# Third weight pair behind attention's tail, casts and subtractions a block apart, expert weights landing over w_out's tiles

## The chip, the cores and the metric

One core of a Trainium2 chip runs the whole program. The metric is device microseconds of one execution, as the median of several. A profiled execution shows every engine: TensorE (PE; its weight loads are PEld), VectorE (DVE), ScalarE (ACT), GpSimd (POOL), SyncE (SP, which here only issues DMAs) and the 16 DMA engines.

## The reference

Three layers follow each other. Talking-heads attention (2 batches, 12 heads, 448 tokens, 64 wide) mixes the heads before and after the softmax; a gated feed-forward follows an RMS norm; a mixture of 8 experts with one expert per token ends it.

```python
scores = einsum('bhij,hg->bgij', scale * q @ k.T, w_pre)
attn   = einsum('bhij,hg->bgij', softmax(scores), w_post);  x = attn @ v      # [896, 768]
xn     = x / sqrt(mean(x*x) + 1e-6) * rms_g
x      = (silu(xn @ w_gate) * (xn @ w_val)) @ w_out                           # 768 -> 1536 -> 768
e      = argmax(x @ moe2_w_gate)
out    = gate * eom * (relu(x @ w1[e]) @ w2[e])                               # 768 -> 1024 -> 768
```

The feed-forward's weights are float64 in memory, everything else float32.

## The kernel before

Each large product is made of three fp32r matmuls: an operand is split into a high part (a cast on ScalarE) and a low part (a subtraction on VectorE that needs the cast), and high·high, high·low and low·high are added up in PSUM (`mm3`, lines 502 to 504).

**Attention** (`Attention.run`) walks over 90 blocks of 10 query rows by 12 heads, in 8 chunks. A step m of the loop does this: `pre(m)` (L172, PE) mixes the heads of a tile d that a DMA has shuffled out of the scores (`shuffle`, L166, issued five blocks ahead, from SP for even and from POOL for odd blocks); L176 (DVE) takes the row maximum; `soft` (L182, ACT) the exponential; `weigh(m-1)` (L189 to L191, DVE) scales the second mixing matrix; `post(m-2)` (L202, PE) mixes again and L204 (ACT) copies the result. Between them lie the score products of the next chunk (L157), the products with v (`av`, L216, copied to xT by L222), the norm of a finished chunk (L433 to L455), the loads of v of batch 0 (blocks 0, 2, .. 10) and of k of batch 1 (blocks 12 to 23), both issued from POOL, and whatever `beside` holds for a block. This order is written out by hand (`manual_schedule`); each engine runs its instructions in that order. What follows attention is laid out by a planner, which puts each instruction into its engine's queue by its own estimate of the time at which its inputs are there, and which may also put later work between attention's instructions.

**`beside`** holds the first weights. The weights of the feed-forward come in 12 pairs (gate and value, one pair fc = 128 of the 1536 columns). `f64_to_f32` turns a raw tile into float32: a DMA (L488), a shift (L489, DVE), an and-or (L490, DVE), a scaling (L493, ACT), a shift-or (L494, DVE). `split_one` (L526 cast, L527 subtraction) splits it. Pair 0 is done at blocks 58 to 67, pair 1 at 69 to 78, and at block 79 the DMAs of pair 2 are issued (`load_2`) into the raw tiles that pair 1 has left. The other steps of pair 2 are traced after attention, ahead of `ffn1(0, 1)`. At blocks 83 to 86 `split_x` (L475 cast, L476 subtraction) splits the first four chunks of the normed tokens.

**The tail** of attention has the last `av` products, the norm of the last chunk, the split of chunks 4 to 7, and as filling four products of the feed-forward that need only chunks 0 to 3 and pairs 0 and 1 (`fill`).

**The feed-forward** runs `ffn1(fc, g)` for 12 pairs by two groups of 448 tokens, then `ffn2` for seven tiles of 128 tokens against w_out, of which twelve raw tiles (`wor`) have been converted and split: pieces 0 and 1 live in `nw`, 2 and 3 in `w2p`, 4 to 7 in `w0`, 8 and 9 in `nw`, 10 and 11 in four of the `wor` tiles. `route` then does for each tile: transposes of y (L627), logits (L631), the argmax and a running count (L636 to L668 on DVE, L641 and L643 on PE), and a scatter of the tokens to `ys` (L670, POOL). For the last tile, `first_x` (L776) begins expert 0's transposed tokens out of what `ys` holds by then (`xe`, loaded on ACT's queue after the scatter before), and adds the last tile's own tokens with a picking matmul (L784) after the count.

**The experts**: eight steps of `mm1` and `mm2`. A weight comes as eight pieces of 768 KB (`feed`, L849, SP); 14 raw tiles (`raws`) take them in turn; `weights` casts (L865, ACT) and subtracts (L866, DVE) them. The memory of `raws`, `hi` and the rest is the memory that the feed-forward leaves. The pools lie one above the other in the order in which they are opened, in KB per partition: `nw` 24, `h0` 18, `h384` 12, `h640` 12, `wor` 36, `w2p` 12, `hs` 24, `y` 18; above `nw` the experts' pools begin again at the bottom: before the change raw0 to raw4 (3, 2, 2, 6 and 1 tiles of 6 KB), then `hi` (6 tiles). A load waits until the tiles below it have been read for the last time, and the planner puts it into SP's queue by when the pools below it are free, not by its turn.

Of the kernel before, what the change touches and what calls it, by code (L numbers as in the profile page):

```python
# [20 lines left out]
class Attention:  # L21
# [230 lines left out]
    def run(self):  # L252
        NCH, NB, SH, LP = len(self.chunks), len(self.blocks), self.SH, self.LP
        self.prologue()
        loads = {2 * j: f for j, f in enumerate(self.load_kv(0, "v"))}
        loads.update({j + 12: f for j, f in enumerate(self.load_kv(1, "k"))})
# [59 lines left out]
class Net:  # L316
# [152 lines left out]
    def split_x(self, t0, ni):  # L469

        nc, x = self.nc, self.xT[:, :, t0:t0 + ni]
        g = int(t0 >= self.groups[1][0])
        o = t0 - self.groups[g][0]
        xh, xl = (self.xs[g][:, j, :, o:o + ni] for j in range(2))
        nc.scalar.copy(xh, x)  # L475
        nc.vector.tensor_sub(xl, x, xh.bitcast(F32))  # L476
# [45 lines left out]
    def split_one(self, fc, f, nm, eng):  # L522

        t = (self.nw if fc % 2 else self.w0).tile([128, 2, self.KD, 128], F32R, tag="w" + nm, name=nm + "hl")
        h, l = t[:, 0], t[:, 1]
        self.nc.scalar.copy(h, f)  # L526
        eng.tensor_sub(l, f, h.bitcast(F32))  # L527
        return h, l

    def split_w(self, fc, ws):  # L530
        return [self.split_one(fc, f, nm, self.LO(self.nc)) for f, nm in zip(ws, "gv")]
# [89 lines left out]
    def route(self, t, y):  # L621
# [8 lines left out]
        for k in range(self.KD):  # L630
            nc.tensor.matmul(lg, lhsT=yT[:, k, :], rhs=self.rw[:, k, :], start=(k == 0), stop=(k == self.KD - 1))  # L631
        v, col = nc.vector, lambda j: m[:, j:j + 1]
# [282 lines left out]
    def run(self):  # L915
# [17 lines left out]
        def at(m, f):  # L933
            beside.setdefault(m, []).append(f)

        def first_weights(fc, slots, load=True):

            def begin():
                steps, fs = self.load_w(fc)
                for js, some, f, nm in zip(slots, steps, fs, "gv"):  # L940
                    some = some + [lambda f=f, nm=nm: ws[fc].append(self.split_one(fc, f, nm, nc.vector))]
                    for m, s in zip(js, some):
                        at(m, s)
            return begin

        def begin_x(g):
            self.xs.append(sp[g].tile([128, 2, self.KD, self.groups[g][1]], F32R, tag="s", name=f"x{g}"))
# [10 lines left out]
        def tail(avs, todo):  # L958
# [3 lines left out]
            late = [lambda c=c: self.split_x(c[0] * a.S + c[1], c[2]) for c in a.chunks[-4:]]  # L962

            def gen():
                n = 0
                while todo:
                    yield todo.pop(0)
                yield lambda: begin_x(1)
                yield from late[:3]
                yield from avs[:3]  # L970
                yield fill[0]
                yield from avs[3:]
                yield fill[1]
                steps = [s for s in todo]
# [5 lines left out]
                yield late[3]  # L980
            return gen()

        with ExitStack() as actx:
# [4 lines left out]
            at(57, first_weights(0, ((58, 61, 62, 63, 64, 65), (60, 63, 64, 65, 66, 67))))  # L988
            at(68, first_weights(1, ((69, 73, 74, 74, 75, 76), (70, 75, 76, 76, 77, 78))))
            at(79, load_2)  # L990
            at(80, lambda: begin_x(0))
            for j, c in enumerate(a.chunks[:4]):
                at(83 + j, lambda c=c: self.split_x(c[0] * a.S + c[1], c[2]))
# [18 lines left out]
        for some in raw2.pop():  # L1012
            for f in some:
                f()
# [41 lines left out]
        part = self.first_x(xs[0])  # L1056
        self.route(self.TT - 1, y)
# [7 lines left out]
        self.raws = []  # L1065
        for i, n in enumerate((3, 2, 2, 6, 1)):
            self.raws += [self.pool(m2, f"raw{i}", n)] * n
        self.raws = self.raws[7:13] + self.raws[:7] + self.raws[13:]
        self.nraw = 0
        self.hi = self.pool(m2, "hi", self.NHL)  # L1070
# [93 lines left out]
```

## Time and profile before

| | us |
|---|---|
| median of 3 runs | 786.6 (786.15 to 787.62) |
| profiled execution | 786.7 |
| its span | 785.0 |
| TensorE busy | 730.8 (93%) |
| VectorE busy | 479.8 (61%) |
| ScalarE busy | 387.5 (49%) |
| GpSimd busy | 78.0 (10%) |

By 40 slices of 19.6 us, the lines of the page that carry most (a digit is the busy share in tenths; PEclk the granted clock; DMA the busy share of 16 engines):

| | slices |
|---|---|
| PE | 7889999999998759999999998999988799999994 |
| DVE | 3555667566775775788888823032106889778750 |
| PEclk | 9999999999999799999999999999998899999998 |

A row of a timeline has the start, the duration, the engine, the line, the operation with output and inputs, and in brackets how long the engine had been idle and what ended that. A releaser is inferred from semaphore events. Busy time of TensorE is modelled at its end, since matmuls are pipelined.

### The profile page before, as it was taken

The numbers are of one execution on the slowest core, as the hardware profiler recorded it, in microseconds if no ns is written. First come the engines' busy times: TensorE is split into PE (matmuls) and PEld (weight loads), VectorE is DVE, ScalarE is ACT, GpSimd is POOL, SyncE is SP. The second block draws the span as 40 slices with busy tenths as digits, with TensorE's granted clock in tenths as the row PEclk, the third lists the DMA queues.
The fourth block names the chain that finished last, engine by engine and source line by source line (L and its number), as shares of the span: only waits on it lengthen the run. The fifth ranks groups of instructions, "written<-read, shape, count | busy, mean of one in ns | idle before, by whom it ended". The sixth has DMA issues, their size and how long they took to land.

```text
span 785.0 us, 11939 instructions
## 1 busy us (share of the span) xinstructions
PE 730.8 (93%) x4414; PEld 596.0 (76%) x4414; DVE 479.8 (61%) x1016; ACT 387.5 (49%) x679; POOL 78.0 (10%) x133
## 2 busy tenths in 40 slices
PE   7889999999998759999999998999988799999994
PEld 4456575665645538999999998999986688988894
DVE  3555667566775775788888823032106889778750
ACT  3455656556565453534334512232215777778661
POOL 5133100121001000000000000011000000020010
PEclk9999999999999799999999999999998899999998
DMA  8577755667566404795554000131159999999100
GB/s 136 105 157 147 121 73 82 120 121 173 86 145 113 86 5 161 205 284 195 185 176 163 1 1 0 45 138 61 41 192 387 378 380 381 380 342 355 58 25 17
DMA packets 83434, 122.02 MB, mean 155 GB/s; under 512 B 20915, under 2 KB 63559, under 8 KB 83375
## 3 DMA queue, kind: packets, MB, share of 16 engines
q1 hardware_dynamic: 75471, 98.05, 42.8%
q0 software_dynamic: 6752, 20.05, 12.3%
q10 hardware_dynamic: 1152, 3.15, 1.1%
q8 instruction: 36, 0.59, 0.3%
q14 instruction: 23, 0.19, 0.1%
HBM read 90.51 MB, written 12.21 MB: 131 GB/s over the span
## 4 chain that ended last, share of the span: by engine, by line
PE 66%; DMA 11%; DVE 9%; issue 7%; ACT 5%; POOL 0%; SPq 0%; POOLq 0%; DVEq 0%; ACTq 0%
PE ps_po L202 7%; PE ps_pm L172 6%; PE ps_pm L504 5%; PE ps_pm L502 5%; PE ps_pm L503 5%; PE ps_po L504 5%; PE ps_po L503 5%; PE ps_po L502 5%; PE ps_qk L157 4%; PE ps_av L216 4%; PE ps_qk L503 3%; PE ps_qk L504 3%; PE ps_qk L502 3%; DMA d<-s 3%; DMA xe<-ys 2%
## 5 line engine op out<-in xcount | busy, mean ns | idle before, releaser
L202 PEld LDWEIGHTS ps_po<-w,p 120*112 120x112 f32 x720 | 84.7, 180 | 68.6 <-issue 41.9
L866 DVE TENSOR_TENSOR wl<-raw,wh 128x1536 fp32r<-128x1536 f32 x64 | 110.9, 1754 | 28.2 <-ACT wh L865 28.1
L202 PE MATMUL ps_po<-w,p 120*112 120x120 f32 x720 | 94.9, 276 | 18.4 <-DVE w L191 17.1
L182 ACT ACTIVATE p<-ps_pm,mx 120x448 f32<-120x448 f32 x90 | 57.1, 634 | 102.9 <-DVE mx L176 62.0
L865 ACT CAST wh<-raw 128x1536 fp32r<-128x1536 f32 x64 | 93.0, 1481 | 7.6 <-PE ps_pm L504 4.7
L172 PE MATMUL ps_pm<-d,a_kpre 120*120 120x448 f32 x180 | 86.8, 564 | 4.9 <-DMA d<-s 4.9
L176 DVE TENSOR_REDUCE mx<-ps_pm 120x1 f32<-120x448 f32 x90 | 56.0, 622 | 49.7 <-PE ps_pm L172 49.0
L493 ACT ACTIVATE raw<-raw 128x768 f32<-128x768 f32 x36 | 33.0, 922 | 70.8 <-DVE raw L490 64.0
L204 ACT COPY at<-ps_po 112x480 f32<-112x480 f32 x90 | 50.9, 566 | 3.3 <-PE ps_po L202 1.1
L157 PE MATMUL ps_qk<-kt,qt 64*110 64x448 f32 (+2 forms) x192 | 52.1, 589 | 0.5 <-ACT qt L88 0.2
L503 PE MATMUL ps_po<-wl,hh 128*128 128x384 f32 x144 | 49.4, 343 | 0.3 <-DVE wl L866 0.2
L502 PE MATMUL ps_po<-wh,hh 128*128 128x384 f32 x144 | 49.2, 342 | 0.0
L504 PE MATMUL ps_po<-wh,hl 128*128 128x384 f32 x144 | 48.6, 340 | 0.1
L502 PE MATMUL ps_pm<-wh,xh 128*128 128x512 f32 x108 | 44.9, 416 | 3.0 <-ACT xh L828 2.2
L166 POOL DMA_DIRECT2D d<-s x42 | 24.7, 589 | 218.5 <-PE ps_pm L172 173.6
L504 PE MATMUL ps_pm<-wh,xl 128*128 128x512 f32 x108 | 44.1, 410 | 2.2 <-DVE xl L829 2.2
L216 PE MATMUL ps_av<-at,v 112*64 112x110 f32 (+2 forms) x768 | 45.0, 264 | 1.2 <-ACT at L204 0.7
L503 PE MATMUL ps_pm<-wl,xh 128*128 128x512 f32 x108 | 44.4, 411 | 1.5 <-DVE wl L866 1.5
L597 DVE TENSOR_TENSOR hl<-h,hh 128x1536 fp32r<-128x1536 f32 (+2 forms) x9 | 12.3, 1400 | 48.6 <-ACT hh L596 24.6
L216 PEld LDWEIGHTS ps_av<-at,v 112*64 112x64 f32 x768 | 37.0, 137 | 6.0 <-ACT at L204 0.9
L88 DVE COPY s<-ps_qk 110x448 f32<-110x448 f32 (+2 forms) x48 | 29.8, 622 | 14.8 <-PE ps_qk L157 13.8
L157 PEld LDWEIGHTS ps_qk<-kt,qt 64*110 64x110 f32 (+2 forms) x192 | 15.3, 174 | 30.5 <-issue 22.6
(258 smaller groups left out, 1589.1 us busy)
## 6 DMA issues: line engine op xcount, KB each, us to landing
raw<-in_moe_w_dram SPq DMA_DIRECT2D x64, 768.0 KB
d<-s SPq DMA_DIRECT2D x48, 210.0 KB
raw<-in_moe_w_gate_dram SPq DMA_DIRECT2D x12, 768.0 KB
raw<-in_moe_w_val_dram SPq DMA_DIRECT2D x12, 768.0 KB
raw<-in_moe_w_out_dram SPq DMA_DIRECT2D x12, 768.0 KB
d<-s POOLq DMA_DIRECT2D x42, 210.0 KB, 5.6
ys<-z SPq DMA_DIRECT2D x8, 385.0 KB
v<-in_v_dram POOLq DMA_DIRECT2D x12, 224.0 KB, 6.5
```

What stands on the lines that cost most here:

```text
L157: nc.tensor.matmul(pss[e][:ni], lhsT=self.qt[n][e * D:(e + 1) * D, p, :ni], rhs=self.kt[b, p][e * D:(e + 1) * D, :], start=True, stop=True,)
L172: self.marks[m, "p"] = nc.tensor.matmul(ps, lhsT=self.kpre.rearrange("p i g -> p (i g)"), rhs=self.dt.pop(m), start=True, stop=True).ins
L176: self.marks[m, "v"] = nc.vector.tensor_reduce(mx, ps, axis=AX.X, op=ALU.max, negate=True).ins
L182: self.nc.scalar.activation(p, ps, AF.Exp, bias=mx, scale=1.0, accum_out=sm)
L202: nc.tensor.matmul(ps[:, c], lhsT=p[:, c * CP:(c + 1) * CP], rhs=w, start=True, stop=True)
L204: self.marks[m + self.LP, "a"] = nc.scalar.copy(dst, ps.rearrange("p c h i -> p (c h) i")).ins
L216: nc.tensor.matmul(ps[e * D:(e + 1) * D, j, :ni], lhsT=vt[(g0 + e) // HH][:self.CP, (g0 + e) % HH, c, :], rhs=at[:, c, g0 + e, :ni], start ...
L502: nc.tensor.matmul(ps, lhsT=ah, rhs=bh, start=first, stop=False)
L503: nc.tensor.matmul(ps, lhsT=ah, rhs=bl, start=False, stop=False)
L504: self.last["t"] = nc.tensor.matmul(ps, lhsT=al, rhs=bh, start=False, stop=last).ins
L865: self.nc.scalar.copy(h, raw)
L866: self.last["v"] = self.nc.vector.tensor_sub(l, raw, h.bitcast(F32)).ins
```

## The change

- v's loads of batch 0 move from blocks 0, 2, .. 10 to 6, 8, .. 16; k's loads of batch 1 from blocks 12 to 23 to blocks 7, 9, .. 17 and 19 to 24.
- In `beside`, the cast of a weight and its subtraction stand in two consecutive blocks; pair 1's value ends at block 79. The split of the first four chunks is made likewise.
- In the tail the casts and subtractions of chunks 4 to 7 are spread between the products.
- The conversion of pair 2 is ordered on ScalarE behind the last cast and on VectorE behind the last subtraction of the tokens' split.
- In the last `route`, `first_x` runs behind the logits, not ahead of the transposes.
- The experts' pools: `hi` first, then raw0 to raw6 with 1, 2, 2, 2, 4, 2 and 1 tiles, used in the order 4, 0, 1, 2, 5, 3, 6. So expert 0's w1 lands over eight `wor` tiles (two of which hold w_out's piece 10), its w2 over the rest of `h0`, `h384` and the first half of `h640`, expert 1's w1 over `h640`, `w2p` and `wor`.

```diff
@@ -252,8 +252,9 @@
         self.prologue()
-        loads = {2 * j: f for j, f in enumerate(self.load_kv(0, "v"))}
-        loads.update({j + 12: f for j, f in enumerate(self.load_kv(1, "k"))})
+        loads = {2 * j + 6: f for j, f in enumerate(self.load_kv(0, "v"))}
+        for j, f in enumerate(self.load_kv(1, "k")):
+            loads[2 * j + 7 if j < 6 else j + 13] = f
         avs, todo, preps = [], [], []
...
@@ -472,8 +473,14 @@
         xh, xl = (self.xs[g][:, j, :, o:o + ni] for j in range(2))
-        nc.scalar.copy(xh, x)
-        nc.vector.tensor_sub(xl, x, xh.bitcast(F32))
+
+        def high():
+            self.last["xa"] = nc.scalar.copy(xh, x).ins
+
+        def low():
+            self.last["xv"] = nc.vector.tensor_sub(xl, x, xh.bitcast(F32)).ins
+
+        return high, low
...
@@ -523,12 +530,16 @@
         h, l = t[:, 0], t[:, 1]
-        self.nc.scalar.copy(h, f)
-        eng.tensor_sub(l, f, h.bitcast(F32))
-        return h, l
+        return [lambda: self.nc.scalar.copy(h, f), lambda: eng.tensor_sub(l, f, h.bitcast(F32))], (h, l)
...
     def split_w(self, fc, ws):
-        return [self.split_one(fc, f, nm, self.LO(self.nc)) for f, nm in zip(ws, "gv")]
+        out = []
+        for f, nm in zip(ws, "gv"):
+            steps, hl = self.split_one(fc, f, nm, self.nc.vector)
+            for s in steps:
+                s()
+            out.append(hl)
+        return out
...
@@ -618,7 +629,7 @@
-    def route(self, t, y):
+    def route(self, t, y, beside=None):
         nc, E, rp = self.nc, self.E, self.rp
...
@@ -629,6 +640,8 @@
             nc.tensor.matmul(lg, lhsT=yT[:, k, :], rhs=self.rw[:, k, :], start=(k == 0), stop=(k == self.KD - 1))
+        if beside:
+            beside()
         v, col = nc.vector, lambda j: m[:, j:j + 1]
...
@@ -938,8 +951,12 @@
                 for js, some, f, nm in zip(slots, steps, fs, "gv"):
-                    some = some + [lambda f=f, nm=nm: ws[fc].append(self.split_one(fc, f, nm, nc.vector))]
-                    for m, s in zip(js, some):
+                    def split(f=f, nm=nm, m=js[6]):
+                        (high, low), hl = self.split_one(fc, f, nm, nc.vector)
+                        ws[fc].append(hl)
+                        high()
+                        at(m, low)
+                    for m, s in zip(js, some + [split]):
                         at(m, s)
...
@@ -959,25 +976,31 @@
                     for fc, j, tag in ((0, 0, "qk"), (0, 1, "qk"), (1, 0, "qk"), (1, 1, "pm"))]
-            late = [lambda c=c: self.split_x(c[0] * a.S + c[1], c[2]) for c in a.chunks[-4:]]
+            def late(c):
+                return self.split_x(c[0] * a.S + c[1], c[2])
...
             def gen():
-                n = 0
                 while todo:
                     yield todo.pop(0)
-                yield lambda: begin_x(1)
-                yield from late[:3]
+                begin_x(1)
+                cs = [late(c) for c in a.chunks[-4:]]
+                yield cs[0][0]
+                yield cs[1][0]
                 yield from avs[:3]
+                yield cs[0][1]
                 yield fill[0]
+                yield cs[1][1]
                 yield from avs[3:]
+                yield cs[2][0]
+                yield cs[2][1]
                 yield fill[1]
-                steps = [s for s in todo]
+                steps = list(todo)
                 k = [s.__name__ for s in steps].index("mean") + 1
...
                 yield from steps[k:]
-                yield late[3]
+                yield from cs[3]
             return gen()
...
@@ -985,12 +1008,16 @@
             self.NCH = len(a.chunks)
-            at(57, first_weights(0, ((58, 61, 62, 63, 64, 65), (60, 63, 64, 65, 66, 67))))
-            at(68, first_weights(1, ((69, 73, 74, 74, 75, 76), (70, 75, 76, 76, 77, 78))))
+            at(57, first_weights(0, ((58, 61, 62, 63, 64, 65, 66), (60, 62, 63, 64, 65, 66, 67))))
+            at(68, first_weights(1, ((69, 73, 74, 75, 76, 77, 78), (70, 74, 75, 76, 77, 78, 79))))
             at(79, load_2)
...
             for j, c in enumerate(a.chunks[:4]):
-                at(83 + j, lambda c=c: self.split_x(c[0] * a.S + c[1], c[2]))
+                def split(c=c, j=j):
+                    high, low = self.split_x(c[0] * a.S + c[1], c[2])
+                    high()
+                    at(84 + j, low)
+                at(83 + j, split)
             with tc.manual_schedule():
...
@@ -1009,9 +1036,11 @@
             self.ffn1_out(fc, 0, early[fc, 0], early[fc, 1])
-        for some in raw2.pop():
-            for f in some:
-                f()
+        steps = raw2.pop()
+        with tc.issue_after(self.last["xa"]), tc.issue_after(self.last["xv"]):
+            for some in steps:
+                for f in some:
+                    f()
         self.ffn1(0, 1, ws[0])
...
@@ -1053,8 +1082,8 @@
         y, = self.ffn2(ts, hs)
-        part = self.first_x(xs[0])
-        self.route(self.TT - 1, y)
+        part = []
+        self.route(self.TT - 1, y, lambda: part.extend(self.first_x(xs[0])))
         self.warm(self.NW[2], self.last["t"])
...
@@ -1062,12 +1091,10 @@
         m2 = ExitStack()
-        self.raws = []
-        for i, n in enumerate((3, 2, 2, 6, 1)):
-            self.raws += [self.pool(m2, f"raw{i}", n)] * n
-        self.raws = self.raws[7:13] + self.raws[:7] + self.raws[13:]
+        self.hi = self.pool(m2, "hi", self.NHL)
+        self.raws = [[self.pool(m2, f"raw{i}", n)] * n for i, n in enumerate((1, 2, 2, 2, 4, 2, 1))]
+        self.raws = [p for i in (4, 0, 1, 2, 5, 3, 6) for p in self.raws[i]]
         self.nraw = 0
-        self.hi = self.pool(m2, "hi", self.NHL)
         self.xp = self.pool(m2, "xp", 2)
...
```

## Rows read from the trace of the kernel before

**Rows 1.** The page: the chain that ended last, by engine.

```profile
PE 66%; DMA 11%; DVE 9%; issue 7%; ACT 5%; POOL 0%; SPq 0%; POOLq 0%; DVEq 0%; ACTq 0%
```

**Rows 2.** Stages: us, PE PEld DVE ACT POOL busy, granted clock, DMA share, GB/s.

```profile
250.30:263.40 13.10, 5.40 (x24) 3.71 (x23) 6.71 (x14) 4.85 (x10) 0.58 (x1) 0.64 0.57 156
263.40:274.80 11.40, 10.87 (x127) 8.71 (x127) 7.82 (x25) 5.87 (x15) 1.15 (x2) 0.96 0.43 53
274.80:293.20 18.40, 10.47 (x62) 6.63 (x60) 13.54 (x40) 10.17 (x25) 0.00 (x0) 1.00 0.03 5
330.60:425.00 94.40, 94.40 (x468) 87.52 (x467) 80.30 (x121) 37.93 (x50) 0.00 (x0) 1.00 0.65 204
596.30:626.00 29.70, 23.72 (x107) 20.07 (x108) 26.83 (x27) 22.11 (x22) 1.73 (x1) 0.89 1.05 380
626.00:775.00 149.00, 148.26 (x784) 132.60 (x783) 108.52 (x126) 101.67 (x112) 13.00 (x8) 0.99 0.72 258
```

**Rows 3.** Timeline of TensorE, first blocks: start, us, line, operation, idle before and releaser.

```profile
37.41 0.98 PE L172 MATMUL ps_pm<-d,a_kpre 120*120 120x448 f32 x2 [0.15 <-DMA d<-s]
42.24 1.72 PE L172 MATMUL ps_pm<-d,a_kpre 120*120 120x448 f32 x2 [3.03 <-DMA d<-s]
```

**Rows 4.** Chain of waits, the same stretch: start, us, what.

```profile
31.45 10.66 DMA d<-s
```

**Rows 5.** DMA issues: queue, count, KB each, median us to landing.

```profile
v<-in_v_dram POOLq DMA_DIRECT2D x12, 224.0 KB, 6.5
k<-in_k_dram POOLq DMA_DIRECT2D x18, 112.0 KB, 6.5
```

**Rows 6.** Timeline of TensorE, attention's later blocks.

```profile
247.58 1.04 PE L202 MATMUL ps_po<-w,p 120*112 120x120 f32 x8 [0.51 <-DVE w L191]
250.31 0.98 PE L202 MATMUL ps_po<-w,p 120*112 120x120 f32 x8
259.75 1.91 PE L202 MATMUL ps_po<-w,p 120*112 120x120 f32 x8 [7.70 <-DVE w L191]
263.37 1.40 PE L202 MATMUL ps_po<-w,p 120*112 120x120 f32 x8
```

**Rows 7.** Timeline of VectorE, the same stretch.

```profile
256.32 0.56 DVE L489 TENSOR_SCALAR raw<-raw 128x768 uint32<-128x768 uint32 x1 [6.91 <-DMA raw<-in_moe_w_gate_dram]
```

**Rows 8.** Waits in 205 to 296 us: us in total, times, longest.

```profile
DVE x L476 <- ACT x L475: 5.2, 3, 2.2
```

**Rows 9.** VectorE by line, 200 to 430 us: busy us, mean ns.

```profile
L490 DVE SCALAR_TENSOR_TENSOR raw<-raw 128x768 uint32<-128x768 uint32 x35 | 33.3, 955 | 0.5
```

**Rows 10.** Timelines at attention's end: VectorE, then TensorE.

```profile
314.83 0.83 DVE L476 TENSOR_TENSOR x<-xT,x 128x648 fp32r<-128x648 f32 x1 [0.80 <-ACT x L475]
316.02 0.36 PE L502 MATMUL ps_pm<-x,ghl 128*128 128x448 f32 x1
```

**Rows 11.** Timeline of ScalarE and TensorE, from the last w_out tile to routing.

```profile
583.54 0.49 ACT L616 ACTIVATE y<-ps_po 128x384 f32<-128x384 f32 x1 [5.71 <-PE ps_po L504]
586.42 0.94 PE L776 MATMUL ps_pm<-ident,xe 128*128 128x128 f32 x6 [2.92 <-DMA xe<-ys]
588.92 1.51 PE L631 MATMUL ps_av<-rw,yT 128*128 128x16 f32 x12 [0.24 <-ACT yT L628]
591.41 0.17 PE L641 MATMUL ps_qk<-oh,tri 128*128 128x8 bf16 x1 [0.98 <-DVE oh L639]
```

**Rows 12.** Chain of waits: the load of expert 0's tokens.

```profile
578.88 7.50 DMA xe<-ys
```

**Rows 13.** Timeline of SyncE's queue, w_out's last matmuls.

```profile
577.80 0.37 SPq L849 DMA_DIRECT2D raw<-in_moe_w_dram  x1
583.53 0.90 SPq L849 DMA_DIRECT2D raw<-in_moe_w_dram  x2
```

**Rows 14.** Timeline of ScalarE, the first experts' start.

```profile
594.83 1.48 ACT L865 CAST wh<-raw 128x1536 fp32r<-128x1536 f32 x1
604.19 0.60 ACT L882 ACTIVATE h<-ps_pm 128x512 f32<-128x512 f32 x1 [3.39 <-PE ps_pm L504]
```

## The prediction, made before the changed kernel was seen

> **What bounds the kernel now.** I read the page's chain first, then the busy time by stage, then the timelines of the stretches that the diff touches. By the chain [rows 1] the end is TensorE's for two thirds, and it waits for DMAs for a tenth. By stage [rows 2] TensorE has no free time where no edit lies: it is busy for 94.40 of 94.40 us in the feed-forward (330.6 to 425) and for 148.26 of 149.00 among the later experts. So microseconds saved ahead of such a stage come out at the end, unless a feeder turns late. TensorE does idle where the edits lie: in the first blocks, at attention's blocks 80 to 89, and between the last w_out tile and the first expert. The stages [rows 2] show for the second of these 5.40 us busy of 13.10, then 10.87 of 11.40, then 10.47 of 18.40.
>
> **Part a, loads of v and k.** TensorE stands for 3.03 us ahead of pre(6) and then does it in 1.72 where pre(5) took 0.98 [rows 3]: 3.03 + 0.74 = 3.8 us. The transfer awaited took 10.66 us [rows 4]; issued in block 1, it shared the engines with the v loads of blocks 2 and 4 (224 KB each, 448 KB [rows 5]). These move behind block 6, so up to 3.8 us go. In return, blocks 6 to 11, which have three v loads before and after, get three k loads of 112 KB, 336 KB. If 448 KB cost 3.03 us of wait, 336 KB cost at most 3.03 x 336 / 448 = 2.3; they may be hidden altogether, since a block's d is asked for five blocks ahead. Bounds: a gain of 3.8, a loss of 2.3. I take 3.8 less two thirds of 2.3, 2.3 us. POOL's queue, past which these loads move, carries only its d shuffles there; v is first read in block 18, two blocks after its last load. The trace shows that a k load lands no sooner than a v load of twice the bytes (6.5 and 6.5 us [rows 5]). If k's 336 KB therefore count as 672, the cost is 3.03 x 672 / 448 = 4.5 and the term 3.8 - 4.5 = -0.7; that is in rival 3. The Trainium skill, "DMA: Bandwidth & Descriptors", section Specifications, has a rule of this kind: transfers under 512 B miss line rate, and a piece of k here is 64 floats, 256 B; by it the term would be the -0.7, and the equal landing times agree with it.
>
> **Part b, casts and subtractions of pairs 0 and 1.** A subtraction queued behind the same block's cast holds VectorE and, behind it, the scaling for which post waits. The post at 247.58 waited 0.51 us for that [rows 6]. Four such pairs: 0 to 2.0 us; I take 1.0. The added block costs only one block more of a raw tile's life; pair 2's value DMA waits for block 79's subtraction, with SP's d of block 86 behind it, needed seven blocks on.
>
> **Part c, pair 2's conversion out of attention.** The largest term. post starts at 250.31, and next at 259.75 after 7.70 us idle, and at half the granted clock, then at 263.37 [rows 6]; the clock of 250.3 to 263.4 is 0.64 on average [rows 2], so part of it was at the 1.2 GHz level after the idle time. The cause is one row of VectorE: L489 of pair 2 sat 6.91 us at the head of the queue for its DMA, the block's maxima and scalings behind it [rows 7]. Behind the tail that instruction cannot stand there. From 250.31 to 263.37 two blocks took 13.06 us; the block before took 250.31 - 247.58 = 2.73. Gain 13.06 - 2 x 2.73 = 7.6; bounds 6.9 (the wait alone) and 8.6 (blocks without the 0.51 wait). What is next late is the usual loop of maximum, exponential and scaling, which 2.73 contains.
>
> **Part d, blocks 81 to 83.** Pair 2's other steps go too, but each block here carries two av products and TensorE is busy for 10.87 of 11.40 us [rows 2]: 0 to 0.5, I take 0.4.
>
> **Part e, the first four chunks' split.** From 274.8 to 293.2 VectorE is busy 13.54 of 18.40 us and TensorE 10.47 [rows 2]. Three subtractions waited 5.2 us for their casts [rows 8], with the next maximum behind them. A block apart, VectorE becomes the limit: at most 18.40 - 13.54 = 4.9. Some of its idle time is the loop through ScalarE and stays: bounds 1 and 4.9, I take 3.2.
>
> **Part f, the tail and the feed-forward's start.** Pair 2 costs VectorE two shifts and four steps like L490 [rows 9], 2 x 0.56 + 4 x 0.955 = 4.9 us, and now comes after the last subtraction of the tokens (314.83 + 0.83 [rows 10]). Cover: from 316.02 [rows 10] TensorE does ffn1(0,1) and ffn1(1,1), 72 matmuls; at 468 in 94.40 us [rows 2] that is 14.5 us. In these VectorE has to do 4.9 plus two subtractions like L490, 1.9, together 6.8, and outputs. It is busy for 80.30 of 94.40 us later [rows 2], so the debt can be paid back within 33 us. Cost 0; without the cover 4.9. The spread casts of chunks 4 to 7 lie beside the filling products: 0. The last chunk's subtraction ends at 315.66, 0.36 us before it is needed, so the tail can neither gain nor lose much.
>
> **Part g, transposes behind logits.** After the last eviction of y (583.54 + 0.49 = 584.03) TensorE waits for xe until 586.42, and only then come first_x, transposes and logits (done at 588.92 + 1.51 = 590.43) and the count at 591.41 [rows 11]. first_x is 12 matmuls; transposes and logits then take 590.43 - 588.02 = 2.4 us if first_x ended 1.6 us after 586.42. Changed: transposes at 584.03, logits done at 586.4, first_x from then to 588.0, the count directly behind it, since its one-hot is ready 0.98 after the logits. 591.41 - 588.05 = 3.3 us; 4.0 if the planner puts the count first. xe took 7.50 us from its issue at 578.88 on [rows 12], on ACT's queue, beside the raw loads that SP had issued from 577.80 on [rows 13]. With the changed pools w2p's two loads and one of `wor` start in about these microseconds, three instead of two. A raw tile of 786 KB at 380 GB/s [rows 2] is 2.1 us. Low end 3.3 - 2.1 = 1.2. The Trainium skill, "DMA: Bandwidth & Descriptors", section Issuing engines are not separate DMA queues, says that a DMA started by ACT interleaves with SP's on the same 16 engines; by it the term would be the 1.2, and the 7.50 us agree that ACT's queue gives no way past.
>
> **Part h, expert weights.** SP's order in the trace is telling: the third expert load waited until 577.80 for w_out's piece 0, and expert 0's first pieces came behind it, most from 583.53 on [rows 13], though some of the memory was free long before. So I expect five loads ahead of ffn2's end over h0, h384 and h640, two over w2p, and expert 0's w1 again at about 583.5. That suffices: the first cast starts at 594.83 [rows 14], 591.5 after part g, and four tiles land at 2.1 us each by about 593; the fourth is cast last. Expert 0's w2 is there sooner, but ScalarE's cast of it stood behind the eviction of h at 604.19, idle for 3.39 us [rows 14], by the planner's order. I take 0; bounds -2.1 (the first pieces a tile later) and +3.4 (the idle time filled).
>
> **The sum.** 2.3 + 1.0 + 7.6 + 0.4 + 3.2 + 3.3 = 17.8 us. The profiled execution has 786.7 (span 785.0 and 1.7 around it), so 768.9; the median of the runs is 0.1 lower: 768.8.
>
> **Rivals.** (1) More: parts a and e at their upper ends and part h's idle time filled, 1.5 + 1.7 + 3.4 = 6.6 more, 762.2. For it: prefetched w2. Against: the order of casts is the planner's. Chance 0.10. (2) Pair 2 comes late: VectorE does other pairs' steps first, the cover fails, 4.9 us and a slow restart like 0.74 come back: 774.4. For it: 85% busy VectorE. Against: 14.5 us of cover for 6.8. Chance 0.13. (3) DMAs give back: part a -0.7 (a k load as dear as a v load), part g 1.2 (a third raw load beside xe), part h -2.1 (first pieces a tile later): 17.8 - 3.0 - 2.1 - 2.1 = 10.6, 776.0. For it: the k row [rows 5] and engines full at 380 GB/s [rows 2]; against: all three have to come. Chance 0.07. (4) It does not do what it says: the planner, laying out anew, puts another waiting step between the blocks, and b, c and e pay nothing: 6.0 less pair 2's 4.9 leaves 1.1, 785.5. Against: no other raw tile has its memory before attention's v is read. Chance 0.04. (5) Slower: VectorE, entering the feed-forward 4.9 us late, evicts products late throughout. Each of the 40 remaining groups of 18 matmuls would wait for an output queued behind one conversion step (0.955); at 0.6 us each that is 24 us, 786.6 + 6.2 = 792.8. It decides from 17.8 / 40 = 0.45 us per group. Against: 14 us of idle VectorE in 94. Chance 0.08.
>
> **Chances and range.** The forecast, 764 to 774, has 0.58. The range 761 to 779 takes in rivals 1 to 3 and the bounds of a, e and h. Faster by over 0.2% (about what a measurement of this kernel can tell from no change): forecast and rivals 1 to 3, 0.88; within 0.2%: rival 4, 0.04; slower: rival 5, 0.08.
>
> **What would show it.** Changed, pre(6) waits less than 1 us and blocks 6 to 11 show no wait for d (a); no idle time of several us on TensorE at block 80, and no L489 waiting for a DMA ahead of attention's last post (c); subtractions L476 without waits for L475 (e); attention's last post some 14 us earlier and ffn1 still without idle time (f); the count about 4.0 us after the last eviction of y, not 7.4 (g); seven expert loads issued before ffn2 ends (h). The prediction is wrong if TensorE idles where pair 2 is needed, if d waits reappear in blocks 6 to 17, or if the experts begin no sooner after the count.

## The result, and the profile after

The changed kernel takes 758.2 us (754.6 to 759.0); the kernel before, timed beside it, takes 787.0 (786.2 to 787.6). The ratio is 0.9626, interval 0.9593 to 0.9659. The profiled execution has 759.0 with a span of 757.3, so 27.7 us less than the span before. The forecast was 768.8, range 761 to 779: the direction was right, the size was 10 us short.

From the page after, the busy time and the chain by engine, which answers to [rows 1]:

```profile
PE 724.7 (96%) x4414; PEld 592.6 (78%) x4414; DVE 478.1 (63%) x1016; ACT 387.8 (51%) x679; POOL 77.3 (10%) x133
PE 72%; issue 9%; DMA 9%; DVE 7%; ACT 2%; POOL 0%; POOLq 0%; SPq 0%; DVEq 0%; ACTq 0%
```

TensorE does the same 4414 instructions as before. Of the 27.7 us, 21.6 are idle time of TensorE that went and 6.1 are busy time (730.8 before, 724.7 now); the mean granted clock is 0.989 against 0.975. The view by stages after, bounded by the same instructions as far as [rows 2] has them (post(77) to post(79), to post(82), to post(88), the feed-forward, the first expert, the rest; columns as there). The bound between the last two rows is not the same instruction as before; the table further down measures that stretch.

```profile
248.45:253.24 4.79, 3.83 (x24) 2.44 (x22) 4.45 (x11) 3.12 (x8) 1.12 (x2) 1.00 0.82 185
253.24:264.31 11.07, 10.54 (x126) 8.38 (x127) 5.84 (x23) 5.52 (x16) 0.60 (x2) 1.00 0.69 166
264.31:278.45 14.14, 10.28 (x62) 6.62 (x60) 13.27 (x40) 9.95 (x25) 0.00 (x0) 1.00 0.04 7
315.84:410.25 94.41, 94.41 (x468) 87.52 (x467) 82.40 (x125) 39.08 (x51) 0.00 (x0) 1.00 0.63 205
576.52:599.79 23.27, 21.58 (x106) 18.75 (x104) 21.71 (x26) 19.87 (x21) 0.00 (x0) 0.93 1.06 381
599.79:747.00 147.21, 147.04 (x788) 132.33 (x786) 113.34 (x132) 104.19 (x113) 13.84 (x9) 1.00 0.75 272
```

The first row was 13.10 us at a clock of 0.64 and is 4.79 at 1.00. The third was 18.40 and is 14.14, with VectorE busy for 13.27 of it: that engine is now the limit there. The feed-forward is unchanged, TensorE without idle time. The fifth row is the one that the prediction did not foresee: before, the first expert's stretch had 23.72 us of TensorE's work in 29.70, now 21.58 in 23.27.

The same in TensorE's timeline, for [rows 6] and [rows 11]: the posts behind the vanished stall, then the last tile's first_x and the count.

```profile
250.03 1.02 PE L202 MATMUL ps_po<-w,p 120*112 120x120 f32 x8
253.24 0.94 PE L202 MATMUL ps_po<-w,p 120*112 120x120 f32 x7 [0.84 <-DVE w L191]
568.34 0.49 PE L789 MATMUL ps_pm<-ident,xe 128*128 128x128 f32 x2 [0.44 <-DMA xe<-ys]
572.50 0.17 PE L654 MATMUL ps_qk<-oh,tri 128*128 128x8 bf16 x1 [0.98 <-DVE oh L652]
```

The post that waited for 7.70 us waits for nothing, the next one for 0.84, and the tokens' wait of 2.92 is 0.44.

Every other number on stages is the distance between the starts of the same two instructions in the timelines, TensorE's except for the eviction of y, which is ScalarE's. pre(m) and post(m) are block m's two mixings; "y to count" runs from the start of y's last eviction (583.54 before) to the count (591.41); "e0 to e1" from expert 0's first matmul (596.35) to the first matmul of the ninth group of expert 1's first product (631.50).

| run | pre 64 to 78 | pre 78 to 82 | pre 82 to post 89 | y to count | e0 to e1 |
|---|---|---|---|---|---|
| before | 41.8 | 20.3 | 27.7 | 7.9 | 35.2 |
| changed | 39.4 | 10.9 | 23.5 | 4.9 | 27.6 |
| changed_again | 39.4 | 10.9 | 23.5 | 4.4 | 27.0 |
| hold_alone | 41.8 | 14.5 | 27.7 | 7.2 | 35.1 |
| spacing_alone | 39.4 | 10.9 | 31.8 | 7.2 | 36.4 |
| new_pools_alone | 41.8 | 21.1 | 27.7 | 4.7 | 26.6 |
| pairs_close | 41.8 | 14.4 | 24.3 | 4.4 | 26.6 |
| pair2_free | 39.4 | 10.9 | 27.7 | 4.4 | 26.5 |
| tokens_close | 39.4 | 10.9 | 27.7 | 4.4 | 26.3 |
| first_x_early | 39.4 | 10.9 | 23.6 | 4.7 | 27.6 |
| early_loads | 39.4 | 10.9 | 23.5 | 4.4 | 27.6 |
| old_pools | 39.4 | 10.9 | 23.5 | 6.9 | 35.1 |
| old_pools_hold13 | 39.4 | 10.9 | 23.8 | 6.2 | 31.7 |
| old_pools_hold12 | 39.4 | 10.9 | 24.0 | 6.3 | 29.1 |
| old_pools_tokens_first | 39.4 | 10.9 | 23.5 | 6.4 | 28.7 |
| tokens_late | 39.4 | 10.9 | 23.5 | 4.4 | 28.8 |

The 27.7 us of the two profiled executions, in order: the start to pre(14) lost 1.2 (59.5 to 60.7), of which 1.9 lie ahead of pre(0), where nothing was edited (27.70 and 29.55), while pre(0) to pre(14) gained 0.6; pre(64) to post(89) gained 16.0; the tail and the feed-forward nothing (21.94 and 162.71 in both); the entry into w_out's products 1.1, which is the clock; y to count 3.0; from there to expert 0 0.9; e0 to e1 7.5; the rest 0.4.

### The profile page after: what moved, and what is told of

It is laid out like the page before. It is cut to its first block, busy times and chain, and to the rows that moved or that the text cites. A ratio compares the mean times of both kernels' runs of the same rounds, so it can differ in the third digit from the quotient of the medians.

```text
span 757.3 us, 11947 instructions
## 1 busy us (share of the span) xinstructions
PE 724.7 (96%) x4414; PEld 592.6 (78%) x4414; DVE 478.1 (63%) x1016; ACT 387.8 (51%) x679; POOL 77.3 (10%) x133
## 4 chain that ended last, share of the span: by engine, by line
PE 72%; issue 9%; DMA 9%; DVE 7%; ACT 2%; POOL 0%; POOLq 0%; SPq 0%; DVEq 0%; ACTq 0%
PE ps_po L202 8%; PE ps_pm L172 7%; PE ps_pm L511 6%; PE ps_pm L509 5%; PE ps_pm L510 5%; PE ps_av L216 5%; PE ps_po L511 5%; PE ps_po L509 5%; PE ps_po L510 5%; PE ps_qk L157 5%; DMA out_dram<-o,ids 4%; PE ps_qk L510 3%; PE ps_qk L511 3%; PE ps_qk L509 3%; DMA d<-s 2%
## 5 line engine op out<-in xcount | busy, mean ns | idle before, releaser
L879 DVE TENSOR_TENSOR wl<-raw,wh 128x1536 fp32r<-128x1536 f32 x64 | 110.9, 1753 | 21.6 <-ACT wh L878 21.5
L608 DVE TENSOR_TENSOR hl<-h,hh 128x1536 fp32r<-128x1536 f32 (+2 forms) x9 | 12.3, 1400 | 47.4 <-ACT hh L607 24.6
L88 DVE COPY s<-ps_qk 110x448 f32<-110x448 f32 (+2 forms) x48 | 29.8, 622 | 17.1 <-PE ps_qk L157 16.7
L157 PEld LDWEIGHTS ps_qk<-kt,qt 64*110 64x110 f32 (+2 forms) x192 | 15.2, 179 | 30.1 <-issue 24.0
```

The lines of the kernel that those rows point to most:

```text
L157: nc.tensor.matmul(pss[e][:ni], lhsT=self.qt[n][e * D:(e + 1) * D, p, :ni], rhs=self.kt[b, p][e * D:(e + 1) * D, :], start=True, stop=True,)
L879: self.last["v"] = self.nc.vector.tensor_sub(l, raw, h.bitcast(F32)).ins
```

## The experiments

Medians scatter: those of the kernel before, timed beside each batch, lie between 785.4 and 787.9. Where medians lie within 2 us of each other I go by the stages above, and say so.

**Pools undone in the changed kernel, and pools alone in the kernel before.**

```diff
-        self.hi = self.pool(m2, "hi", self.NHL)
-        self.raws = [[self.pool(m2, f"raw{i}", n)] * n for i, n in enumerate((1, 2, 2, 2, 4, 2, 1))]
-        self.raws = [p for i in (4, 0, 1, 2, 5, 3, 6) for p in self.raws[i]]
+        for i, n in enumerate((3, 2, 2, 6, 1)):
+            self.raws += [self.pool(m2, f"raw{i}", n)] * n
+        self.raws = self.raws[7:13] + self.raws[:7] + self.raws[13:]
+        self.hi = self.pool(m2, "hi", self.NHL)
```

> The changed kernel with the experts' pools laid out as before (raw0 to raw4 with 3, 2, 2, 6 and 1 tiles, hi above them); all else as changed. The changed kernel has 758.2 us. In its trace the stretch from the first expert's first matmul to the end is some 7.7 us shorter than before, where the prediction had 0. Theory order: the layout only makes the planner put expert 1's tokens (their transposes, casts and subtractions) ahead of a block of weight casts, so that TensorE neither waits twice for 2.2 us at expert 1's start nor falls to half clock there. Theory loads: the gain comes from weights that land earlier. Both expect the 7.7 us to be lost again: 765 to 767 us, with two waits of about 2 us on TensorE at expert 1's start. Theory elsewhere: the experts gained from the earlier scatter and routing, not from the pools: 758 to 760 us.

Measured 767.4 (765.5 to 768.6): 9.2 us lost.

> The kernel before (787.0 us) with only the experts' pools laid out as changed. Theories order and loads: the 7.7 us of the experts' stretch are gained alone, 778.5 to 780.5 us, with expert 1's tokens ahead of the casts and no wait of 2 us at its start. Theory elsewhere: within 1 us of the kernel before. A third outcome, more than 9 us gained, would say that the pools also pay ahead of the experts (routing).

Measured 776.5 (773.8 to 776.7) beside 787.9: 11.3 us gained, the third outcome. The pools are the largest part of the change, and they pay at two places: e0 to e1, and y to count. For the second, the chain of waits of the changed kernel:

```profile
559.59 3.47 DMA ys<-y,sl
563.08 5.22 DMA xe<-ys
```

The load of expert 0's tokens takes 5.22 us, not 7.50 [rows 12]. With the old pools two raw loads go out in the microsecond before it (558.90 and 559.37, the load itself at 559.71, in old_pools; 577.80 and 578.27 before, of which [rows 13] shows the first). With the new ones it is one, 0.2 us ahead (562.91 and 563.08), and in new_pools_alone none (579.53 against 579.37). The Trainium skill, "DMA: Bandwidth & Descriptors", section Issuing engines are not separate DMA queues, lets loads of all issuers interleave on the same engines; the two durations agree with that, and so do the other old-pool traces in which TensorE waits for this load (7.0 to 7.2 us). That the loads just ahead are the cause is read from the traces; no run changes them alone.

**Order or landing?** The same pools, once with expert 1's tokens ordered ahead, once with the new pools and the tokens ordered late.

```diff
 # old_pools_tokens_first, on top of old_pools
+        self.WB.update({n: ("ta", "tv") for n in (10, 11, 12, 13)})   # casts, subtractions behind the tokens'
+                if first and k0:                                        # expert 0's second product, second half
+                    s.enter_context(self.tc.issue_after(self.last["tp"]))
 # tokens_late, on the changed kernel
+                if p == 0:
+                    with tc.issue_after(self.last["t"]):
+                        nxt = self.transpose_x(xs[1], 1)
```

> As old_pools, and with an order written out for expert 1's tokens: the second half of expert 0's second product stands behind their transposes on TensorE, and casts and subtractions 10 to 13 of the weights stand behind theirs. Theory order: most of the 7.7 us comes back (the 5.5 us at expert 1's start), 759.5 to 761.5 us, no wait at expert 1's start. Theory loads: nothing comes back, 765 to 767 us or more, since TensorE or the casts then wait for weights or for the load of the tokens instead.

Measured 761.2 (758.5 to 761.9): 6.2 of the 9.2 us come back without any change of memory (1.5 of them in expert 0's first product, ahead of the edit, where the clock is 0.81 against 0.67 in old_pools).

> The changed kernel with the new pools, and expert 1's tokens ordered late on purpose: their transposes behind all of expert 0's second product, as the kernel before has them; the loads are as changed. Theory order: 4 to 6.5 us are lost against the changed kernel (762 to 764.7 us), with TensorE waiting for the tokens' cast and subtraction at expert 1's start. Theory loads: at most 1.5 us are lost, since weights are early either way.

Measured 756.6 (754.9 to 759.2), as much as changed_again in the same batch (756.7). By the stage 1.8 us are lost (28.8 against 27.0), not the expected 4 to 6.5, so my theory, as I had put it, fell: late transposes on TensorE are at most a small part of the cause. What differs shows on ScalarE. old_pools first, then tokens_late, then the changed kernel (timeline: casts of weights, evictions, then the cast of the tokens, L841):

```profile
591.10 8.36 ACT L878 CAST wh<-raw 128x1536 fp32r<-128x1536 f32 x6
599.37 0.58 ACT L920 ACTIVATE o<-ps_po,mt 128x384 f32<-128x384 f32 x1
599.84 0.86 ACT L841 CAST xh<-ps_qk 128x512 fp32r<-128x512 f32 x2
```

```profile
587.62 4.25 ACT L878 CAST wh<-raw 128x1536 fp32r<-128x1536 f32 x3
591.76 0.59 ACT L920 ACTIVATE o<-ps_po,mt 128x384 f32<-128x384 f32 x1
592.23 1.49 ACT L878 CAST wh<-raw 128x1536 fp32r<-128x1536 f32 x1
593.60 0.60 ACT L920 ACTIVATE o<-ps_po,mt 128x384 f32<-128x384 f32 x1
594.07 0.88 ACT L841 CAST xh<-ps_qk 128x512 fp32r<-128x512 f32 x2
```

```profile
592.18 1.50 ACT L878 CAST wh<-raw 128x1536 fp32r<-128x1536 f32 x1
593.57 0.87 ACT L841 CAST xh<-ps_qk 128x512 fp32r<-128x512 f32 x2
```

With the old pools six casts stand in a row and thirteen in all ahead of the tokens. With the new ones it is nine in the changed kernel, and twelve, broken up, in tokens_late. So the next theory was the queue, not the place on TensorE:

```diff
 # on top of old_pools; hold12: (12, 13)
+        self.WB.update({n: ("ta", "tv") for n in (13,)})
```

> As old_pools (767.4 us), and the thirteenth cast and subtraction of the experts' weights (the first of expert 1's second matrix) stand behind the cast and subtraction of expert 1's tokens; nothing is ordered on TensorE. In old_pools ScalarE has thirteen casts ahead of those tokens, six of them in a row (8.36 us), and VectorE thirteen subtractions; in tokens_late, where nothing was lost, it is twelve. Theory queue: one cast (1.48 us) and one subtraction (1.75 us) less ahead of the tokens take most of the two waits of 2.22 and 1.30 us at expert 1's start and the half clock behind them: 762.5 to 765 us. Theory loads: the time of the casts is set by the weights' landing, nothing comes back, 766.5 to 768 us.

> As old_pools_hold13, with the twelfth cast and subtraction behind the tokens too. Theory queue: no wait of over 1 us is left at expert 1's start unless its own last weights come late; 760.5 to 763.5 us, as old_pools_tokens_first (761.2), though the transposes stay late on TensorE. Theory loads: 766.5 us or more.

Measured 765.7 (765.0 to 768.1) and 763.7 (761.3 to 767.6). Both medians lie 0.2 to 0.7 us off the expected bounds, high; between 767.4 and 763.7 the ranges overlap, so the stages decide: e0 to e1 falls from 35.1 to 31.7 and to 29.1. The waits of TensorE at expert 1's start show why, old_pools above, hold12 below:

```profile
600.48 0.79 PE L509 MATMUL ps_pm<-wh,xh 128*128 128x512 f32 x1 [2.22 <-ACT xh L841]
603.85 0.80 PE L511 MATMUL ps_pm<-wh,xl 128*128 128x512 f32 x1 [1.30 <-DVE xl L842]
```

```profile
600.10 0.50 PE L510 MATMUL ps_pm<-wh,xh 128*128 128x512 f32 x1 [0.46 <-ACT xh L842]
601.96 0.50 PE L512 MATMUL ps_pm<-wh,xl 128*128 128x512 f32 x1 [0.23 <-DVE xl L843]
```

In the first, the matmuls start at half clock as well (0.79 us each where the second has 0.50). Holding back two casts and two subtractions gives 6.0 of the 7.5 us, while no order was set for the transposes and the loads stay late. Of these 6.0, 1.2 lie in expert 0's first product, ahead of the edit, and are the clock there (0.81 against 0.67). From the start of expert 0's second product to the end of e1, where the edit acts, old_pools has 21.8 us, hold13 19.9, hold12 17.1 and the changed kernel 15.0: the queue makes 4.8 of 6.8 us. The Trainium skill, "TensorE: Matmul & The Clock Gate", section Architectural detail: the array is 16× 32×32, not 1× 128×128, says that ScalarE and VectorE take their queues strictly in order; these rows agree.

**Pair 2 and the pairs' spacing**, each undone in the changed kernel and each alone in the kernel before. Some conversion steps of the pairs move by a block with the spacing (their block numbers are left out of the cut), so the two are tested together.

```diff
 # pair2_free: without the order        # hold_alone: this order alone, in the kernel before
-        with tc.issue_after(self.last["xa"]), tc.issue_after(self.last["xv"]):
 # pairs_close: cast and subtraction in one block      # spacing_alone: a block apart, in the kernel before
-                        at(m, low)
+                        low()
```

> The changed kernel without the order that holds pair 2's conversion behind the tail; the planner puts it where it wants. Theory (the prediction's part c): it comes back between attention's last blocks, its first shift sits at the head of VectorE's queue for its DMA, TensorE idles for 6 to 8 us at block 80 and runs at half clock after: 758.2 + 8.5 = 766.7, between 765 and 768 us. Rival: with casts and subtractions a block apart VectorE has so much room that the conversion costs little, 759 to 761 us; the order matters little then.

Measured 759.8 (758.3 to 763.7): the rival's time. The stall is gone from pre(78) to pre(82) even so. The planner now puts the first shift behind the next maximum and scaling, where it waits for less (VectorE, pair2_free):

```profile
253.52 0.56 DVE L496 TENSOR_SCALAR raw<-raw 128x768 uint32<-128x768 uint32 x1 [1.97 <-DMA raw<-in_moe_w_gate_dram]
```

What the order behind the tail is worth then shows one stage on, where VectorE is the limit: 23.5 becomes 27.7.

> The changed kernel with cast and subtraction of weight pairs 0 and 1 in one block again (pair 1's value ends at block 78); pair 2 still held behind the tail. In the trace of the changed kernel the spacing gained 2.4 us at blocks 65 to 70 and 0.7 at block 77, where the prediction had 1.0 for all. Theory wait (the subtractions waited 1.5 and 2.7 us, the prediction took one post's 0.51): 758.2 + 3.1 = 761.3, between 760 and 762.5 us, and no stall at block 80. Theory place (the spacing, not the order behind the tail, takes pair 2's stall away, as pair2_free suggests): the stall at block 80 returns as well, 768 to 770 us.

Measured 766.4 (760.7 to 768.9), between the two theories: 2.4 us at pre 64 to 78 as expected, and 3.4 more at pre 78 to 82.

> The kernel before (785 to 788 us) with only pair 2's conversion ordered behind the tail; casts and subtractions of the pairs stay in one block. Theory of the prediction (part c): all of the stall at block 80 goes, 8.5 us from block 78 to block 82, 778 to 780 us. Theory two waits (from pairs_close): behind the shift that waits 6.91 us for its DMA stands the subtraction of pair 1's value, which would have waited 2.6 us for its cast anyway; 5.9 us go and a wait of 2.2 us stays ahead of a post, 780 to 782.5 us.

Measured 779.0 (775.5 to 782.7) beside 787.7. The median speaks for the first theory, the trace for the second: 20.3 becomes 14.5, not 10.9, and this wait is left (VectorE, hold_alone):

```profile
252.33 0.96 DVE L527 TENSOR_TENSOR vhl<-raw,vhl 128x768 fp32r<-128x768 f32 x1 [2.62 <-ACT vhl L526]
```

It explains 5.8 us of the gain; the others (0.7 at y to count, 1.1 behind it) fall where nothing was edited and are not put down to it.

> The kernel before with only casts and subtractions of pairs 0 and 1 a block apart; pair 2's conversion free. Theory of the prediction (part b): 1 us (0 to 2), and the stall of 7.7 us at block 80 stays: 785 to 787 us. Theory wait: 2.4 us at blocks 65 to 70 and 0.7 at block 77 whatever pair 2 does; and since pair 1 ends a block later the planner puts pair 2's first shift later too, behind the maximum and scaling of a block, so that it waits some 2 us for its DMA, not 6.9 (as in pair2_free): 5 to 9 us gained in all, 777 to 782 us.

Measured 778.1 (777.6 to 781.4) beside 787.7, as the second theory has it. The stall goes wholly (20.3 to 10.9), and 4.1 us come back behind it, in the stretch at whose head pair 2's steps now lie (27.7 to 31.8; VectorE does them from 253.3 to 261.9 us, the tokens' subtractions from 266.9 on).

**The tokens' spacing undone.**

```diff
                     high()
-                    at(84 + j, low)
+                    low()
```

> The changed kernel with cast and subtraction of the first four chunks of the tokens in one block again (blocks 83 to 86). Theory of the prediction (part e, 3.2 us, 1 to 4.9; 4.3 in the trace): 758.2 + 4.3 = 762.5, between 761 and 763.5 us, with waits of the subtraction for its cast, 1 to 2.2 us each. Rival: the gain there came from pair 2's steps being gone from blocks 79 to 83 and ScalarE being early; then at most 1.5 us are lost, under 760 us.

Measured 761.6 (758.6 to 764.2), 3.4 us lost; in the stage 23.5 becomes 27.7, 4.3 us.

**first_x and the loads undone.**

```diff
 # first_x_early
-        part = []
-        self.route(self.TT - 1, y, lambda: part.extend(self.first_x(xs[0])))
+        part = self.first_x(xs[0])
+        self.route(self.TT - 1, y)
 # early_loads
-        loads = {2 * j + 6: f for j, f in enumerate(self.load_kv(0, "v"))}
-        for j, f in enumerate(self.load_kv(1, "k")):
-            loads[2 * j + 7 if j < 6 else j + 13] = f
+        loads = {2 * j: f for j, f in enumerate(self.load_kv(0, "v"))}
+        loads.update({j + 12: f for j, f in enumerate(self.load_kv(1, "k"))})
```

> The changed kernel with first_x ahead of the last tile's transposes again. Theory order (the prediction's part g): the transposes wait for the tokens' load once more, 3.3 us (1.2 to 4.0) are lost, 760 to 762 us. Theory load: with the new pools fewer raw loads are issued just ahead of that load; it takes 5.2 us, not 7.5, and lands about when y is there, so the order is worth at most 0.5 us: 757.7 to 759 us. The trace of new_pools_alone, which has the early first_x and no wait for the tokens, speaks for it.

Measured 759.8 (757.8 to 762.0). The stage says 4.7 against 4.4 to 4.9: the order is worth nothing that can be seen once the pools are new (with the old ones, 0.3 to 0.9: 7.2 against 6.2 to 6.9).

> The changed kernel with v's and k's loads issued where they were before (v in blocks 0 to 10, k in 12 to 23). The prediction gave the move 2.3 us (-2.3 to 3.8). Theory load (the prediction's part a): block 6's tile d shares the engines with v's loads, so the wait ahead of its first mixing grows from 2.58 back to 3 us or more and 1 to 2.5 us are lost: 759 to 761 us. Theory shuffle: the tile's own transfer takes 10.0 us even with no other load beside it in the changed kernel (10.66 before), so the move is worth at most 0.6 us and the time stays at 757.5 to 759; the distance from block 0 to block 14 is 31.2 to 31.8 us either way, unless the clock falls at another point.

Measured 759.0 (758.0 to 761.1), 0.7 above the changed kernel of the first batch and 2.2 above changed_again, which is not more than the scatter. The chain of waits, changed kernel and early_loads:

```profile
33.34 10.00 DMA d<-s
```

```profile
31.93 10.68 DMA d<-s
```

**The changed kernel once more.**

> The changed kernel once more, to see how far its stretches differ between executions: the same order of work, so the distances between events after block 14 should agree within 0.2 us except where the granted clock falls at another place; the start (to block 14) may differ by up to 4 us, as among the runs so far. Median 757 to 760 us.

Measured 756.7 (754.3 to 760.0), 0.3 below the expected bound. The stages of the table agree within 0.1 up to post(89), within 0.7 behind it; the start to pre(14) is 57.3 against 60.7, and the entry into w_out's products 15.2 against 12.3.

## Why the prediction was wrong, point by point

**h, the step that failed.** The prediction took 0 for the experts, with +3.4 as its upper bound, "the idle time filled", and argued against more that "the order of casts is the planner's". It is the planner's, but the planner lays out anew when a pool moves. With the new pools nine casts stand ahead of expert 1's tokens, not thirteen, and 7.5 us went from e0 to e1. All of it went from the start of expert 0's second product on (22.9 us before, 15.0 now); there the queue makes 4.8 of the 6.8 us that the pools are worth in the changed kernel (old_pools_hold12). Weights that come sooner gained nothing at expert 0: nine expert loads are issued before ffn2's last matmul, four before the change, and its first product, up to its ninth group, takes 9.8 us against 9.4. The bound was wrong for a second reason: it was taken from one idle time of ScalarE. The row for the stage, which the text quoted for its GB/s alone, had 29.70 us with TensorE busy for 23.72 at a clock of 0.89 [rows 2], so 6 us idle and a slow clock besides. The same kernel's timeline has 4.4 of them at expert 1's start:

```profile
620.52 0.50 PE L502 MATMUL ps_pm<-wh,xh 128*128 128x512 f32 x1 [2.22 <-ACT xh L828]
623.89 0.79 PE L504 MATMUL ps_pm<-wh,xl 128*128 128x512 f32 x1 [2.18 <-DVE xl L829]
```

Why the planner's estimate tips with the pools was not traced; that it does is shown by new_pools_alone. The remaining 2.0 of the 6.8 us were not taken apart; tokens_late, with its 1.8, points to the place of the transposes, but old_pools_tokens_first, with early transposes, still has 16.9 us there.

**b and c, the right place, the shares wrong.** Together 8.6 were forecast for the stretch that gave 11.8 (2.4 and 9.4). c's step "what is next late is the usual loop" failed. Behind the shift that waited for its DMA [rows 7] stood the subtraction of pair 1's value, which would have waited 2.6 us for its cast in any case (hold_alone). So holding pair 2 back gives 5.8 by itself, and the rest of the stall is the spacing's. b was sized by a post's wait of 0.51, where the subtractions' own waits, up to 2.7 us, were the cost (VectorE, the kernel before):

```profile
219.04 0.96 DVE L527 TENSOR_TENSOR vhl<-raw,vhl 128x768 fp32r<-128x768 f32 x1 [2.70 <-ACT vhl L526]
```

That "the added block costs only one block more of a raw tile's life" missed its use: with the spacing the planner puts pair 2's shift later, and spacing alone removes the whole stall.

**d and e.** e's 3.2 measured 4.3, near its upper bound: VectorE does become the limit (13.27 of 14.14 us). It needs both edits: with the tokens spaced but pair 2 free, or pair 2 held but the tokens close, the stretch stays at 27.7. d's 0.4 did not show: between post(79) and post(82) TensorE is idle for 0.53 us before and after (11.40 less 10.87, 11.07 less 10.54), and the 0.3 us less are busy time, at a clock of 1.00 for 0.96.

**f, right.** The tail and the feed-forward kept their lengths to 0.01 us, so rivals 2 and 5 did not come: the cover held, and no product was evicted late.

**g, the size right by luck, the cause wrong.** Forecast 3.3, measured 3.0. But the transposes' order does not do it: the load of the tokens lands sooner with the new pools, and the early first_x would then run before y is there (first_x_early loses nothing that can be seen). Nor did the order come out as forecast: the planner still puts part of first_x between the transposes (568.34 above). The prediction expected three raw loads beside that load instead of two, where one goes out ahead of it, and so had the sign of this wrong: it charged the pools 2.1 us here, in its lower bound, where they pay 2.5 to 3.2 (7.2 to 7.9 against 4.7).

**a, smaller than forecast, the cause wrong in the main.** Forecast 2.3. The wait ahead of pre(6) went from 3.03 to 2.58 [rows 3], not to the "less than 1 us" that the prediction named as its sign:

```profile
43.48 1.61 PE L172 MATMUL ps_pm<-d,a_kpre 120*120 120x448 f32 x2 [2.58 <-DMA d<-s]
```

The transfer awaited takes 10.00 us in the changed kernel and 9.39 in changed_again, where the first v and k loads go out only in its last 1.4 to 2.4 us (40.95 and 41.64 in the changed kernel); so the expectation of early_loads, "no other load beside it", was not quite right. It takes 10.66 to 10.68 with three v loads under it. A shuffle of the changed kernel that is over before any of these loads goes out takes 8.78:

```profile
23.23 8.78 DMA d<-s
```

Most of it is thus the shuffles' own time, which the prediction had put down to sharing. What the move is worth stays open: the wait ahead of pre(6) is 2.8 to 3.3 us in the five runs with early loads and 1.6 to 3.1 in the eleven with late ones, 0.8 less in the mean, and all waits of 2.0 or less stand where the clock had fallen (0.87 in the mean from pre(0) to pre(6)). That a k load is as dear as a v load, from which rival 3 had -0.7, was not tested apart; no run with late loads waits for d in blocks 7 to 14, where both loads now lie.

**Sum.** 16.0 against 12.2 for b to e, 3.0 against 3.3 for g, 7.5 against 0 for h, -1.2 against 2.3 for a with the scatter of the start, and 2.4 in places where no edit lies. Of the 10 us that were missing h makes 7.5 and the stall behind the stall, with e, 3.8; a took 3.5 of it back. Rival 1, "more", came nearest with 762.2, by e's upper end, but it looked for the experts' part in expert 0's second matrix, not in expert 1's tokens; with a chance of 0.10 and a range that ended at 761 it was not given its weight.

## What to carry to other kernels

Where a planner sets the order, moving memory can move the order: price each stage that it lays out by all of its idle time and its slow clock, not by one wait. Behind an instruction that stands at the head of a queue, look up when the next one's input was ready: the longer wait hides the shorter, and two edits may each remove the same one. And before a transfer's time is put down to its neighbours, look for one of its kind that has none.

## What the runs showed of the hardware

The same order of work took different times in different executions where the granted clock fell. The tail is 21.94 us in the changed kernel and 24.85 in first_x_early, which has the same instructions there:

```profile
279.33:301.27 21.94, 21.15 (x180) 19.01 (x179) 12.44 (x23) 8.82 (x14) 0.28 (x1) 1.00 0.43 144
277.40:302.25 24.85, 23.82 (x181) 21.57 (x179) 12.42 (x23) 8.82 (x14) 0.28 (x1) 0.87 0.37 127
```

Ahead of it, TensorE had been busy for 10.28 of 14.14 us between the posts in the changed kernel, and the two agree there to 0.2 us. After such a stretch the clock fell in some executions and stayed in others, worth 2.9 us (the tail is 24.5 to 24.9 us in three of the sixteen traces, 21.6 to 22.8 in the others); likewise the entry into w_out's products, behind 2.23 us of idle time, 12.3 and 15.2 us in two executions of the changed kernel. A difference of 3 us between two profiles is thus not yet an effect of an edit.

The shuffles keep the DMA engines busy for few bytes: in the changed kernel, from 35 to 40 us, when only shuffles are under way, the engines are busy for 0.69 at 140 GB/s, and for 1.06 at 381 GB/s under the experts' loads.

```profile
35.00:40.00 5.00, 4.75 (x28) 3.27 (x27) 2.64 (x10) 3.46 (x9) 0.58 (x1) 1.00 0.69 140
```
